# Moving the leftover queries' product into the middle of the two-level stretch, and one late sum behind the last quarter

## The chip, the cores and the metric

The kernel runs on one core of a Trainium2 chip. The metric is the device time of one execution in microseconds (us), the median of several runs. A profiled execution shows when each instruction ran on each engine: PE (matrix products; PEld is its weight loading), DVE (vector sums and products), ACT (copies and functions of one argument), POOL[...] and SP (it issues most transfers, as DMA queue).

## The reference

Two blocks follow each other. The first is a linear attention with a norm over each head's 64 values, the second a multiplicative feed-forward network:

```python
kv  = np.einsum('bhsd,bhse->bhde', k, v)
o   = np.einsum('bhsd,bhde->bhse', q, kv)
rms = np.sqrt(np.mean(o * o, axis=-1, keepdims=True) + 1e-06)
o   = o / rms * g_norm
x   = o.transpose(0, 2, 1, 3).reshape(B * S, H * D)
a, b = x @ w1, x @ w2
out = ((a * b) @ w3) @ w_out
```

B = 8 batches, H = 8 heads, S = 576 tokens, D = 64. So x has 4608 rows of 512 columns; w1 and w2 are 512 x 1024, w3 is 1024 x 1024 and w_out 1024 x 512. Everything is float32.

## The kernel before

**Groups.** The 4608 tokens are worked in nine groups of 512. Groups 0 to 7 take the first 512 tokens of batches 0 to 7. The 64 tokens that each batch has beyond 512 are collected into group 8: the *leftover* queries of two batches at a time make one block of 128 rows, so the leftover product is made at each odd batch (1, 3, 5, 7), for that batch and the one before it. The groups run in the order 0 to 6, 8, 7. w3 and w_out are multiplied into one matrix at the start.

**Stages of a group.** While group T is in the network, the attention of batch T+1 is made for the next group, in small pieces between its products. The network's first product (x with w1 and w2) is cut into four blocks of columns, p0 to p3. The matrix products use Strassen's scheme with Winograd's sums: seven products of quarters instead of eight, with sums of quarters made on DVE before and after. In groups 4, 5, 6, 8 and 7 the blocks p0 and p1 are done together with two levels of the scheme (`gates_of_two`, "the stretch of the two levels"): a first half with w1 and a second half with w2, seven outer products of seven matmuls each. The order there is p2, two-level stretch, p3, then the projection (`project_twice`, the product with the folded matrix, also with two levels). A call `between()` after certain products runs the next piece of attention: pieces 0 and 1 in p2, 2 and 3 after the third and the sixth product of the first half, 4 and 5 likewise in the second half, 6 and 7 in p3.

**Memory of the products.** PE writes into eight banks: five in the pool `ps_mm` ("mm") for the network, three in `ps_at` ("at") for the attention. The two-level stretch holds all five of "mm". An outer product fills two banks; of the seven, several accumulate into banks that ACT has copied out (`keep`, L994 and L995) or DVE has added up (`add`, L999 and L1000) just before; `finish` (L1011 to L1016) makes the sums of a quarter.

**Attention pieces.** `begin_kv` (L340) makes the keys' product, `product` (L430) the main queries' product, followed by `norm`: ACT squares (L390), DVE reduces (L399), ACT takes the root (L403), DVE takes the reciprocal (L405) and multiplies (L408). From batch 5 on (`b > FIRST_OF_TWO`) the buffer of the squares is a single one. `product_left` (L449) is the leftover queries' product; its norm has 256 columns instead of 512. `x_left_by_dma` turns the result: POOL copies (L299), a transposing DMA on SP's queue (L301), POOL copies back (L311). The operand of `product_left`, qT_left, comes the same way, with ACT copies, in the slot after the fourth product of the first half.

**Before the change, for batches 5 and 7**, `product_left` is piece 6, in p3 of groups 4 and 6, with one bank of "at" and one of "mm". Its two squares are issued at once into two halves of one buffer; the reduces and the root run when DVE has finished the quarter c12 of p3, the reciprocal and the multiplies behind the quarter c22. For batches 1 and 3 all of the norm runs at once.

**The sums behind p3's quarters.** The quarters c12, c22, c11 and c21 of p3 come in this order (L860, L861; c21 L857). Behind each of them `following` holds the sums that the projection needs. `sum_ab_two` makes four sums for the blocks p0 and p1: two (L1044, L1045) right behind the two-level stretch, the third (L1046, c12 from c11) and the fourth (L1047, called s4) in `following`. `sum_ab` does the same for p3 (L773, L774), and `sum_inner` (L1141 to L1145) makes the second level's sums for the projection's products in turn.

**What sets the order.** PE, POOL and SP run in the order of the program. In p3 and in the projection DVE does as well (in groups 8 and 7 from the two-level stretch on); elsewhere a scheduler places DVE's and ACT's instructions. Each engine works through its own queue in order.

Of the kernel before, what the change touches and what calls it, by code (L numbers as in the profile page):

```python
# [12 lines left out]
FP32 = mybir.dt.float32  # L13
# [3 lines left out]
AF = mybir.ActivationFunctionType  # L17
ALU = mybir.AluOpType
AX = mybir.AxisListType
# [3 lines left out]
def kernel(  # L23
# [32 lines left out]
    nc = tc.nc  # L56
    PSUM = bass.MemoryType.PSUM
    P = 128

    B, H, S, D = q.shape  # L60
# [4 lines left out]
    FIRST_OF_TWO = 4  # L65
    NH = KF // 2
    J = 4
    G = J * P
# [7 lines left out]
    work = ctx.enter_context(tc.tile_pool(name="work", bufs=2))  # L76
    ps_mm = ctx.enter_context(tc.tile_pool(name="ps_mm", bufs=5, space=PSUM))
# [6 lines left out]
    def bank(pool, tag):  # L84
        return pool.tile([P, 512], FP32, name=tag, tag=tag)
# [169 lines left out]
    def all_of(steps):  # L255
        for _ in steps:
            pass
# [63 lines left out]
    def attention(b):  # L321
# [53 lines left out]
            to = st["qT"].rearrange("p r t -> p (r t)")  # L375
            return turn_by_dma([src], to, src, [to], copy or q_copy)

        def norm(o_ps, dsts, squares_first=False):

            n, w = len(o_ps), o_ps[0].shape[1]  # L380
            inv = work.tile([P, n, w // D], FP32, name="inv")
            sq = []

            def square(i):
                if squares_first and i:
                    sq.append(sq[0][:, w:2 * w])
                else:
                    at = 0 if b > FIRST_OF_TWO else i
                    sq.append(work.tile([P, G], FP32, name=f"sq{at}", bufs=1))
                nc.scalar.activation(sq[i][:, 0:w], o_ps[i], AF.Square)  # L390

            if squares_first:
                for i in range(n):
                    square(i)
                yield
            for i in range(n):
                if not squares_first:
                    square(i)
                nc.vector.tensor_reduce(  # L399
                    out=inv[:, i], in_=sq[i][:, 0:w].rearrange("p (h d) -> p h d", d=D), axis=AX.X, op=ALU.add  # L400
                )
            yield
            nc.scalar.activation(inv, inv, AF.Sqrt, scale=1.0 / D, bias=eps_col)  # L403
            yield
            nc.vector.reciprocal(inv, inv)  # L405
            for i in range(n):
                m, k = dsts[i].shape[1:3]
                nc.vector.tensor_tensor(  # L408
                    out=dsts[i],
                    in0=o_ps[i].rearrange("p (m k d) -> p m k d", k=k, d=D),  # L410
                    in1=inv[:, i].rearrange("p (m k) -> p m k", k=k).unsqueeze(3).to_broadcast(
                        [P, m, k, D]
                    ),
                    op=ALU.mult,
                )
# [24 lines left out]
        def product_left():  # L440

            xn = st["left"] = work.tile([P, NP, 2, D], FP32, name="xn_left", bufs=1)

            o_ps = [bank(ps_at, "at"), bank(ps_mm, "mm")]
            for r in range(NP):
                for l in range(2):
                    for e in range(2):
                        rows = slice(e * D, (e + 1) * D)
                        nc.tensor.matmul(  # L449
                            o_ps[e][l * L:(l + 1) * L, r * D:(r + 1) * D],  # L450
                            lhsT=st["qT"][rows, r, l * L:(l + 1) * L],
                            rhs=kv_sb[(b - 1 + l) % 3][rows, e, r, :],
                            start=True,
                            stop=True,
                        )
            o_ps = [t[:, 0:NP * D] for t in o_ps]
            dsts = [xn[:, :, e:e + 1, :] for e in range(2)]
            if b <= FIRST_OF_TWO:
                all_of(norm(o_ps, dsts))
            else:  # L460
                left_norm.append(norm(o_ps, dsts, True))
                next(left_norm[0])

        def turn(r):

# [62 lines left out]
            q_two_by_dma, q_by_dma, q_left_by_dma, x_by_dma, x_part_by_dma, x_left_by_dma, load_ahead,  # L528
        )})

    batches, left_norm = {}, []

    def batch(b):
        if b not in batches:
# [51 lines left out]
    def steps(b):  # L586

        a = batch(b)
        a.start()
        more = b + 1 < B
        fs, ends = ([[] for _ in range(8)] for _ in range(2))

        def turn(i, f, *args, next_group=False):

            t = []

            def begin():  # L600
                t.append(f(*args))
                next(t[0])
                next(t[0])

            fs[i].append((begin,))
            (to_end if next_group else ends[i + 1]).append((lambda: all_of(t[0]),))

        if to_end:

            ends[0] += [(lambda: nc.gpsimd.tensor_copy(tick, late["p5"][:, 0, 0:1]),), *to_end]  # L610
        to_end.clear()
        odd = b % 2
        by_scalar = b > FIRST_OF_TWO
        if b == 1:
            early.extend(a.q_two_by_dma(r) for r in (0, 1))
            q_first = list(early)
            fs[0].append((a.begin_kv, 0, 1))

            def end_first():
                for t in q_first:  # L620
                    with tc.issue_after(copies["kv"].ins):
                        next(t)
                    all_of(t)

            ends[1].append((end_first,))
        fs[1] += [(a.begin_kv, 2, 3), (a.finish, 0)]
        if b == 1:
            last = {}

            def begin(name, behind, f, *args):  # L630
                last[name] = f(*args)
                with tc.issue_after(copies[behind][-1].ins):
                    next(last[name])
                next(last[name])

            def end(name, behind):
                with tc.issue_after(copies[behind][-1].ins):
                    next(last[name], None)
                all_of(last[name])

            fs[2] += [(begin, f"q{r}", "u2", a.q_two_by_dma, r) for r in (2, 3)]
            fs[3] += [
                (begin, "x", "u3", a.x_by_dma, 0, nc.scalar.copy),
                (begin, "left", "u3", a.q_left_by_dma),
            ]
            ends[4] += [(end, "q2", "p1"), (end, "q3", "p5"), (end, "x", "u2")]
            ends[5].append((end, "left", "u3"))
        elif by_scalar:
            turns_by_scalar(b)
        else:  # L650
            turn(1, a.q_two_by_dma, 2, 3)
            turn(2, a.x_by_dma, 0)
            if odd:
                turn(1, a.q_left_by_dma)
        second = 5 if b == 1 else 4
        if more:
            fs[second].append((batch(b + 1).begin_kv, 0, 1))
        fs[second].append((a.finish, 1))
        if odd:
            fs[6 if by_scalar else second].append((a.product_left,))  # L660
        if b == 1:
            turn(6, a.x_by_dma, 1)
            turn(7, a.x_left_by_dma, next_group=True)
        else:
            if not by_scalar:
                turn(5, a.x_by_dma, 1)
            if odd:
                turn(7 if by_scalar else 5, a.x_left_by_dma, next_group=more or by_scalar)
                if by_scalar and not more:
                    slots["proj", "p5"] = [to_end.pop()]  # L670
        if more and not by_scalar:
            turn(7 if b == 1 else 5, batch(b + 1).q_two_by_dma, 0, 1, next_group=True)
        if more:
            fs[7 if odd else 0].append((load_q_left, b + 1))
        return iter([lambda s=e + f: [f(*args) for f, *args in s] for e, f in zip(ends, fs)])
# [728 lines left out]
    for n, T in enumerate(groups):  # L1404
# [29 lines left out]
        for p in range(NF):  # L1434
# [3 lines left out]
            if T and p + 1 == NF:  # L1438
                sum_1, sum_2, sum_4, sum_3 = sum_ab(p)
                following = {  # L1440
                    "c12": [], "c22": [sum_1],
                    "c11": [
                        lambda: sum_inner(0, lambda: all_of(f() for f in (sum_2, sum_3))),
                        lambda: sum_inner(1),
                    ],
                    "c21": [sum_4],
                }

                if T in IN_TWO:
                    following["c12"] += [lambda: all_of(next(t) for t in left_norm for _ in range(2)), *of_two[:1]]  # L1450
                    following["c22"] += [lambda: all_of(left_norm.pop()) if left_norm else None, *of_two[1:]]
                if T not in TWICE:
                    in_order = tc.manual_schedule(engines={mybir.EngineType.DVE})
                    in_order.__enter__()
                gates(T, p, between, lambda name: all_of(f() for f in following[name]))
                continue
# [82 lines left out]
```

## Time and profile before

| | us |
|---|---|
| median of 3 runs | 755.9 (755.87 to 755.94) |
| the profiled execution | 757.01 |
| its span, first to last instruction | 754.9 |
| PE busy in it | 744.5 (99%) |
| DVE busy | 635.8 (84%) |
| ACT busy | 322.4 (43%) |
| POOL busy | 85.2 (11%) |

The granted clock of PE is 1.0 of full speed throughout. The stages of three groups, from the chain of waits and the windows of the trace:

| | two-level stretch | length | DVE busy | ACT busy | p3 and projection |
|---|---|---|---|---|---|
| group 4 (leftover of batch 5) | 407.09 to 431.57 | 24.48 | 19.84 | 20.33 | to 467.91 |
| group 5 (no leftover) | 482.61 to 507.09 | 24.48 | 19.66 | 18.62 | to 541.07 |
| group 6 (leftover of batch 7) | 555.76 to 578.93 | 23.17 | 19.85 | 19.30 | to 615.34 |

Group 6 has no keys' product in that stretch (batch 8 doesn't exist), which is 1.31 us in groups 4 and 5. A line of the chain or of the timeline begins with its start and its length in us; "x24" is a number of records (a float32 matmul leaves two), and "[0.91 <-DVE ab L861]" means that the engine sat idle for 0.91 us and what ended the idle time. Busy time of PE is no proof of full speed, since the ends of matmuls are modelled.

### The profile page before, as it was taken

How to read it: one execution, taken by the hardware profiler on the slowest of the kernel's cores; microseconds unless marked ns; L12 is line 12 of the kernel's file. 1: busy time of each engine (PE TensorE's matmuls, PEld its weight loads, DVE VectorE, ACT ScalarE, POOL GpSimd, SP SyncE). 2: the span in 40 equal slices, each digit the busy share in tenths (PEclk: the TensorE clock that was granted, in tenths of full speed). 3: DMA queues.
4: the chain of work that ended last, by engine and by line, in shares of the span. 5: the costliest groups of instructions: out<-in, count | busy, mean ns of one | idle time of the engine just before them, and what ended most of it. 6: DMA issues, size and time to landing. Idle time of an engine off the chain costs nothing.

```text
span 754.9 us, 15615 instructions
## 1 busy us (share of the span) xinstructions
PE 744.5 (99%) x6155; PEld 659.2 (87%) x6155; DVE 635.8 (84%) x1301; ACT 322.4 (43%) x558; POOL 85.2 (11%) x83
## 2 busy tenths in 40 slices
PE   7999999999999999999999999999999999999998
PEld 5455788888899889988999989999999899999997
DVE  6977999638888669877798899889979897998897
ACT  6777787312322332223225753565367323222321
POOL 0000000222520442053201000100000100000000
PEclk9999999999999999999999999999999999999999
DMA  8996954349997947697578987798656763365354
GB/s 310 344 334 189 273 154 113 85 94 280 329 298 256 251 121 206 227 247 214 151 232 217 267 211 268 207 265 258 250 136 207 190 209 128 147 212 186 121 204 138
DMA packets 155245, 160.94 MB, mean 213 GB/s; under 512 B 87076, under 2 KB 140068, under 8 KB 155172
## 3 DMA queue, kind: packets, MB, share of 16 engines
q1 hardware_dynamic: 152720, 145.52, 65.6%
q10 hardware_dynamic: 2452, 14.42, 5.7%
q8 instruction: 49, 0.80, 0.4%
q14 instruction: 24, 0.20, 0.1%
HBM read 121.90 MB, written 20.71 MB: 189 GB/s over the span
## 4 chain that ended last, share of the span: by engine, by line
PE 91%; DVE 5%; DMA 2%; ACT 1%; issue 0%; SPq 0%; DVEq 0%; ACTq 0%
PE mm L720 42%; PE mm L1183 21%; PE mm L974 15%; PE mm L699 7%; PE at L340 2%; PE at L430 2%; DMA raw<-in_moe_w_out_dram 1%; DVE c L860 1%; PE at L686 1%; DMA raw<-w3o_l 1%; DVE ab L861 1%; DMA raw<-in_moe_w_dram 1%; PE at L1234 0%; DVE inv L399 0%; DVE raw L896 0%
## 5 line engine op out<-in xcount | busy, mean ns | idle before, releaser
L720 PE MATMUL mm<-xT,w_sb 128*128 128x256 f32 x576 | 132.2, 379 | 0.0
L720 PEld LDWEIGHTS mm<-xT,w_sb 128*128 128x128 f32 x576 | 108.7, 190 | 14.8 <-issue 0.5
L720 PE MATMUL mm<-xc,ws 128*128 128x256 f32 x416 | 94.8, 380 | 0.6 <-ACT p L733 0.6
L720 PEld LDWEIGHTS mm<-xc,ws 128*128 128x128 f32 x416 | 78.8, 190 | 12.4 <-ACT p L733 1.8
L699 PE MATMUL mm<-chunks,ab 128*128 128x512 f32 x128 | 60.1, 602 | 1.2 <-DVE chunks L174 1.2
L733 ACT COPY u<-mm 128x512 f32<-128x512 f32 x46 | 27.0, 587 | 74.3 <-PE mm L720 59.6
L733 ACT COPY p<-mm 128x512 f32<-128x512 f32 x54 | 31.5, 586 | 51.5 <-PE mm L720 45.4
L1183 PE MATMUL mm<-w3o_sb,ab 128*128 128x128 f32 x368 | 49.3, 276 | 2.1 <-DVE ab L861 1.9
L720 PE MATMUL mm<-xc,w_sb 128*128 128x256 f32 x208 | 50.0, 383 | 0.0
L1183 PEld LDWEIGHTS mm<-w3o_sb,ab 128*128 128x128 f32 x368 | 45.5, 192 | 3.3 <-DVE ab L861 2.3
L1194 ACT COPY u<-mm 128x512 f32<-128x512 f32 x23 | 13.5, 586 | 81.4 <-DVE raw L1207 48.0
L1183 PE MATMUL mm<-w3o_sb,raw 128*128 128x128 f32 x372 | 48.1, 275 | 0.0
L720 PE MATMUL mm<-xT,ws 128*128 128x256 f32 x192 | 46.0, 382 | 0.0
L1183 PEld LDWEIGHTS mm<-w3o_sb,raw 128*128 128x128 f32 x372 | 44.8, 192 | 0.0
L399 DVE TENSOR_REDUCE inv<-sq 128x8 f32<-128x512 f32 (+1 forms) x40 | 23.9, 627 | 24.5 <-ACT sq L390 24.5
L720 PEld LDWEIGHTS mm<-xc,w_sb 128*128 128x128 f32 x208 | 38.8, 190 | 5.6
L861 DVE TENSOR_TENSOR ab<-c 128x256 f32<-128x256 f32 x78 | 41.3, 529 | 2.1
L699 PEld LDWEIGHTS mm<-chunks,ab 128*128 128x128 f32 x128 | 21.8, 190 | 23.6 <-issue 15.3
L720 PEld LDWEIGHTS mm<-xT,ws 128*128 128x128 f32 x192 | 36.0, 190 | 5.1
L855 ACT COPY c<-mm 128x256 f32<-128x256 f32 x26 | 9.7, 372 | 68.5 <-PE mm L720 68.5
L974 PE MATMUL mm<-ws,w3o_sb 128*128 128x128 f32 x250 | 38.5, 275 | 0.0
L297 POOL COPY xT<-xn 128x1024 uint16<-128x1024 uint16 x14 | 17.3, 1264 | 152.4 <-DVE xn L408 152.4
(249 smaller groups left out, 1630.5 us busy)
## 6 DMA issues: line engine op xcount, KB each, us to landing
w3o_sb<-w3o_l SPq DMA_DIRECT2D x18, 896.0 KB, 5.7
raw<-in_moe_w_dram SPq DMA_DIRECT2D x31, 512.0 KB, 7.2
raw<-w3o_l SPq DMA_DIRECT2D x15, 896.0 KB, 4.9
w3o_sb<-w_l SPq DMA_DIRECT2D x15, 896.0 KB, 5.0
w3o_sb<-w3o_l ACTq DMA_DIRECT2D x14, 896.0 KB, 4.6
k_sb<-in_k_dram SPq DMA_DIRECT2D x32, 256.0 KB, 4.3
v_sb<-in_v_dram SPq DMA_DIRECT2D x32, 256.0 KB, 4.8
q_sb<-in_q_dram SPq DMA_DIRECT2D x32, 256.0 KB, 3.8
```

The lines of the kernel that those rows point to most:

```text
L297: copy(to, src.rearrange("p a n w -> p w a n"))
L340: nc.tensor.matmul(kv_ps[e * D:(e + 1) * D, r - rs[0], :], lhsT=k_sb[:, e, cols] if j < J else kl[:, 2 * r + e, :], rhs=v_sb[:, e, cols] i ...
L399: nc.vector.tensor_reduce(out=inv[:, i], in_=sq[i][:, 0:w].rearrange("p (h d) -> p h d", d=D), axis=AX.X, op=ALU.add)
L430: nc.tensor.matmul(o_ps[l][tokens, n * D:(n + 1) * D], lhsT=qT[r][rows, e, i, tokens], rhs=kv_b[rows, e, r, :], start=True, stop=True,)
L699: nc.tensor.matmul(sums_ps[half][m], lhsT=w3T[half, c][:, m, :], rhs=chunks[:, c, 1, :], start=(c == 0), stop=(c == KF - 1),)
L720: nc.tensor.matmul(ps[:, u, :], lhsT=lhsT(a_name, u, c), rhs=rhs(b_name, c),  start=(u == 0 and c == 0 and to is None), stop=(c == chunks ...
L733: copies.setdefault(name, []).append(nc.scalar.copy(t, ps))
L855: copied = nc.scalar.copy(c, one[:, 0, :])
L861: nc.vector.tensor_mul(dst, c[:, 0, :], c[:, 1, :])
L974: nc.tensor.matmul(ps[place // 4][:, place % 4, :], lhsT=x, rhs=y, start=new and place // 4 not in seen, stop=True, skip_group_check=True,)
L1183: nc.tensor.matmul(to[:, i, :], lhsT=x[:, c, :], rhs=y[:, c, :], start=new and place // 4 not in seen, stop=(c == 1), skip_group_check=True,)
L1194: nc.scalar.copy(t[:, 0:4], ps[0])
```

## The change

1. For batches 5 and 7 `product_left` becomes piece 3, after the sixth product of the first half of the two-level stretch, instead of piece 6. Both its banks are of "at". Its norm runs at once, as for the other batches, and no longer in parts behind c12 and c22; both squares use the same place, so the second waits for the first reduce.
2. `x_left_by_dma` begins at piece 5 instead of 7. Its end is, for batch 5, piece 0 of the next group as before, and for batch 7 piece 6 of the same group instead of a slot in the projection.
3. In groups 4, 5, 6, 8 and 7 the third sum of `sum_ab_two` (L1046) moves from behind c12 to behind c22, and the fourth (L1047) from behind c22 to behind c21, the last quarter.

```diff
-        def norm(o_ps, dsts, squares_first=False):
+        def norm(o_ps, dsts):
 
             n, w = len(o_ps), o_ps[0].shape[1]
             inv = work.tile([P, n, w // D], FP32, name="inv")
-            sq = []
-
-            def square(i):
-                if squares_first and i:
-                    sq.append(sq[0][:, w:2 * w])
-                else:
-                    at = 0 if b > FIRST_OF_TWO else i
-                    sq.append(work.tile([P, G], FP32, name=f"sq{at}", bufs=1))
-                nc.scalar.activation(sq[i][:, 0:w], o_ps[i], AF.Square)
-
-            if squares_first:
-                for i in range(n):
-                    square(i)
-                yield
             for i in range(n):
-                if not squares_first:
-                    square(i)
+                sq = work.tile([P, G], FP32, name=f"sq{0 if b > FIRST_OF_TWO else i}", bufs=1)[:, 0:w]
+                nc.scalar.activation(sq, o_ps[i], AF.Square)
                 nc.vector.tensor_reduce(
-                    out=inv[:, i], in_=sq[i][:, 0:w].rearrange("p (h d) -> p h d", d=D), axis=AX.X, op=ALU.add
+                    out=inv[:, i], in_=sq.rearrange("p (h d) -> p h d", d=D), axis=AX.X, op=ALU.add
                 )
             yield
...
-            o_ps = [bank(ps_at, "at"), bank(ps_mm, "mm")]
+            o_ps = [bank(ps_at, "at"), bank(*((ps_at, "at") if b > FIRST_OF_TWO else (ps_mm, "mm")))]
...
-            dsts = [xn[:, :, e:e + 1, :] for e in range(2)]
-            if b <= FIRST_OF_TWO:
-                all_of(norm(o_ps, dsts))
-            else:
-                left_norm.append(norm(o_ps, dsts, True))
-                next(left_norm[0])
+            all_of(norm(o_ps, [xn[:, :, e:e + 1, :] for e in range(2)]))
...
-            fs[6 if by_scalar else second].append((a.product_left,))
+            fs[3 if by_scalar else second].append((a.product_left,))
...
-                turn(7 if by_scalar else 5, a.x_left_by_dma, next_group=more or by_scalar)
-                if by_scalar and not more:
-                    slots["proj", "p5"] = [to_end.pop()]
+                turn(5, a.x_left_by_dma, next_group=more)
...
                 if T in IN_TWO:
-                    following["c12"] += [lambda: all_of(next(t) for t in left_norm for _ in range(2)), *of_two[:1]]
-                    following["c22"] += [lambda: all_of(left_norm.pop()) if left_norm else None, *of_two[1:]]
+                    following["c22"].append(of_two[0])
+                    following["c21"].append(of_two[1])
```

More of the change, by code (lines that the diff above doesn't have):

```diff
@@ L529, in attention @@
         )})
-    batches, left_norm = {}, []
+    batches = {}
     def batch(b):
```

## The prediction

> **What bounds the kernel now.** I read the page's busy row first: PE is busy 744.5 of 754.9 us, DVE 635.8, ACT 322.4. So only a place where PE waits can give time back. Then the chain of waits, in order of time: in the late groups it is PE without a break, except in two places, 439 to 448 us (group 4) and 587 to 596 us (group 6). These are the two groups that carry the leftover product of an odd batch (5 and 7). Here the chain around the first, and, below the second break, group 5, which carries none (columns: start us, us, what):
>
> ```profile
> 431.57 5.18 PE mm L720 x24
> ...
> 437.38 1.94 PE mm L720 x8
> ...
> 443.47 0.76 DVE xn_left L408 x2
> 444.23 0.60 DVE raw L1047
> ...
> 448.44 19.47 PE mm L1183 x172
> ```
> ```profile
> 507.09 12.09 PE mm L720 x56
> 519.18 21.88 PE mm L1183 x196
> 541.07 4.10 PE mm L720 x19
> ```
>
> The reader should not take the nine microseconds of DVE for a loss: PE works under most of them. Group 5 is the yardstick. From the start of the last block (p3) to the next group it takes 541.07 - 507.09 = 33.98; group 4 takes 467.91 - 431.57 = 36.34, group 6 615.34 - 578.93 = 36.41. The excess is 2.36 + 2.43 = 4.79 us. PE's timeline splits it, group 4 first, then group 5:
>
> ```profile
> 442.59 1.89 PE L720 MATMUL mm<-xc,w_sb 128*128 128x256 f32 x8
> 444.32 0.83 PE L1183 MATMUL mm<-w3o_sb,ab 128*128 128x128 f32 x6
> 446.06 0.94 PE L1183 MATMUL mm<-w3o_sb,ab 128*128 128x128 f32 x6 [0.91 <-DVE ab L861]
> ...
> 448.99 1.28 PE L1183 MATMUL mm<-raw 128*128 128x128 f32 x10
> ```
> ```profile
> 517.29 1.89 PE L720 MATMUL mm<-xc,w_sb 128*128 128x256 f32 x8
> 519.02 1.50 PE L1183 MATMUL mm<-w3o_sb,ab 128*128 128x128 f32 x12
> ...
> 522.14 1.06 PE L1183 MATMUL mm<-raw 128*128 128x128 f32 x8
> ```
>
> The last block's last product starts 442.59 - 431.41 = 11.18 after the block's first matmul in group 4, 517.29 - 506.93 = 10.36 in group 5: the leftover product costs PE 0.82. The projection's first product takes 448.99 - 444.32 = 4.67 against 522.14 - 519.02 = 3.12: a wait of 1.55. It waits for L861 and then for sums that DVE reaches late, since the leftover norm (two reduces, reciprocal, two multiplies) stands before them.
>
> **What the Trainium skill says.** "PSUM — Partial Sum Buffer", section Engine vs sequencer instructions: ScalarE's and VectorE's queues are strict FIFO, and matmuls start and complete in program order. The trace agrees: the leftover squares of group 4 start at 439.21, only when two queue copies (437.32 to 439.31) end. The same page, section PSUM bank collisions, asks that engines be kept apart bank by bank; so a product may enter a bank only when the copy that empties it is done, which decides the second half below. "ScalarE: Activation LUTs", section What ACT_TABLE_LOAD costs, puts a switch of table sets at about 2.66 us; the trace shows none here: Sqrt at 408.35 is followed by a copy at 408.56. "SBUF — State Buffer", section Who interferes with whom: a VectorE operation with two SBUF inputs contends with GpSimd's reads. The trace agrees: L1145 takes 0.88 instead of 0.42 beside the x_left copies at 596.29.
>
> **The change part by part.** The built order shows that, line numbers apart, only the following moves.
>
> *The product.* Its 16 matmuls leave p3 (-0.82 in each of groups 4 and 6) and come between the sixth and seventh product of the first half. There they cost 0.82 again if I take p3's price. The lower bound is the main product's rate, 64 records in 1.09, so 32 in 0.55; nothing below it, since the work stays on the binding engine. I take 0.8. Its operand is ready: the ACT copy of qT_left ends at 414.91, the sixth product at 416.19. So are two banks of the attention pool: the first norm read them until 410.27.
>
> *The norm on ACT.* This is the tight place. ACT between, before the change (group 4):
>
> ```profile
> 414.81 1.99 ACT L297 COPY xT<-xn 128x1024 uint16<-128x1024 uint16 x2
> 417.39 0.59 ACT L994 COPY p<-mm 128x512 f32<-128x512 f32 x1 [0.59 <-PE mm L974]
> 418.06 0.48 ACT L995 COPY p<-mm 128x384 f32<-128x384 f32 x1
> 418.44 1.17 ACT L311 COPY qT<-q_sb 128x1024 uint16<-128x1024 uint16 x1
> 419.50 0.59 ACT L994 COPY u<-mm 128x512 f32<-128x512 f32 x1
> ```
>
> Now both squares stand before the first L994 and Sqrt behind its L995. Both squares share one buffer, so the second waits for the first reduce. First square: PE ends the product near 416.95, square until 417.35. Reduce: DVE has its earlier sums until 417.98, so 417.98 to 418.39. Second square 418.48 (0.09 is the hand-over seen at 406.65). L994 from 418.77, L995 from 419.25, Sqrt 419.62, L311 419.83, and the L994 of the second half's first product 420.89 to 421.48: 1.4 later than before. Behind it waits the second half's third product, which accumulates in that bank. It began at 420.88; pushed by 0.8 it comes at 421.7. Slack 0.2, so I book 0.1 in all; bounds 0 and, if ACT loses another copy's time (0.59), 0.4 in each group. Before that nothing binds: bank 0 is free at 419.4 and needed at about 421.
>
> *The norm on DVE.* Two reduces, reciprocal and two multiplies are 0.33 + 0.33 + 0.2 + 0.34 + 0.34 = 1.5 at their spacing, and some waiting for Sqrt; the second half's first L999 goes from 420.64 to about 422.2. Its bank is next needed at 425.1 + 0.8, by the fourth product. The lag dies at the next norm: DVE idles 1.68 before 425.81 and 0.92 before 427.41. The banks that the next main product needs are free at about 421.2; it comes at 424.5 in group 4, 423.2 in group 6.
>
> *What disappears.* p3 and the projection of groups 4 and 6 get group 5's queues: -0.82 and -1.55 (1.61 in group 6). What is late next there is what binds in group 5: L1145 ends at 521.42 and PE needs it at 521.70, 0.28 of cover. Those are the sums behind c11, and they don't move.
>
> *The late sum, in groups 4 to 8.* L1046 goes from behind c12 to behind c22, L1047 from there to behind c21. c22's L860 waits for PE's fifth product in any case (515.76), so DVE idles 0.6 between and what stands behind c21 comes 0.6 later. Cover: the first of these sums ends at 524.13 and is used at 526.61; the later ones have 1.9 or more. At the end of the kernel DVE's last but one sum starts at 750.27, the last at 751.60 when PE is done: 0.92 idle takes the 0.6. Cost 0; without this cover 0.3 at the end. It can also gain: if a group comes to p3 late on DVE, the 0.6 hole takes the lag up.
>
> *POOL and SP.* POOL's turn copy of xn_left (1.28) starts near 421 instead of 444.44, its DMA transpose stands on SP ahead of the three loads of projection weights, which wait for PE until 428.25; by then POOL is done. So SP isn't held, and the later load of the fourth weights, at 447.76 behind the transpose now, comes earlier. In group 6 POOL's x_left copies (1.65) fall into the second half and slow two or three DVE sums by some 0.4 each; DVE idles 0.92 near there. Cost 0, without cover 0.3.
>
> **Sum.** -4.79 + 1.6 + 0.1 = -3.1. The profiled execution took 757.01, so 753.9; the median lies 1.1 below it: 755.9 - 3.1 = 752.8.
>
> **Rivals.**
> A, the forecast: 752.8; own range 752.2 (product at 0.55 twice: -3.7) to 753.6. For it: group 5 shows the same queues without a wait. 0.72.
> B: ACT's queue slips further and the second half's third product waits 0.5 to 1.2 in each group: 753.8 to 755.2, say 754.3. For it: slack of 0.2 after a chain of seven steps. Against: every step has a duration from a row. 0.13.
> C: DVE doesn't get rid of its lag, and the projection's first product waits as before: 755.9 + 0.1, 756.0. For it: DVE is busy 19.84 of the 24.48 us of the stretch, and 1.5 is added. Against: the idle 2.6 above. 0.09.
> D, slower: the second square waits for the reduce, and behind it on ACT stand the copies that empty the banks. Each microsecond that DVE reaches the first reduce later then moves the third product of the second half, beyond its slack of 0.2. It decides from 1.75 us per group on (the slack and half of 3.1): a second square after 420.2. At 2.6 us, 755.9 - 3.1 + 2 x (2.6 - 0.2) = 757.6. Against: the sums ahead of the reduce are those that end at 417.98 now, and nothing that they wait for moves. 0.06.
>
> **How the numbers follow.** About 0.2% (1.5 us) is what a measurement of this kernel can tell from no change, so faster means below 754.4: A and 0.08 of B, 0.80. Within: the rest of B and C, 0.14. Slower: D, 0.06. The range 752.0 to 754.4 leaves out 0.20.
>
> **What would show it.** Right: in groups 4 and 6 p3 12.09 and the projection 21.88, as in group 5; no wait at L861; the stretch of the two levels 24.48 + 0.8 and 23.17 + 0.8. Wrong: a wait of PE before the second half's third product (B), the wait at the projection's first product still there (C), squares or L994 after 421 (D), or a product whose matmuls cost more than 0.82 in the middle.

## The result and the profile after

| | before | after |
|---|---|---|
| median | 755.92 us (755.70 to 758.03, 6 runs) | 753.10 us (752.18 to 753.69, 6 runs) |
| profiled execution | 757.01 | 753.10 |
| its span | 754.9 | 751.3 |
| group 4, start of p2 to the next group's | 75.52 | 74.05 |
| group 5 | 73.16 | 73.15 |
| group 6 | 74.27 | 72.66 |
| groups 8 and 7, to the start of the last projection | 114.01 | 114.01 |

The ratio of the times is 0.9958, 95% interval 0.9945 to 0.9971: the changed kernel is faster. The groups' lengths are read from the chain of waits as in the prediction. Groups 4 and 6 became 3.08 us shorter together; the span fell by 3.6. Another 0.54 lies ahead of group 4, where the change moves nothing: group 4 starts at 391.85 instead of 392.39, and over all the kernels below, which share their instructions up to there, it starts anywhere between 390.85 and 392.94. So the group lengths, not the spans, are compared from here on. Each is read from one profiled execution. How closely they can be compared is shown by group 5: it takes 73.15 or 73.16 in every kernel below except e6 with two sums. Behind group 6 the kernels differ only in e2 and in e6 with two sums.

The chain of waits after, in groups 4 and 6 (start us, us, what); most lines moved up by some twenty, L720 is L699, L1183 is L1162, L974 is L953 and L449 is L435:

```profile
406.54 9.38 PE mm L953 x84
415.92 0.62 PE at L435 x32
416.54 6.53 PE mm L953 x56
...
431.92 12.09 PE mm L699 x56
444.01 21.88 PE mm L1162 x196
...
563.12 0.62 PE at L435 x32
563.75 6.45 PE mm L953 x56
...
577.73 12.09 PE mm L699 x56
589.82 21.88 PE mm L1162 x196
```

PE's chain has no break. p3 takes 12.09 and the projection 21.88 in both groups, group 5's lengths; the wait for L861 (now L840) in the projection's first product and the wait behind it are gone. In their place the stretch of the two levels has the leftover product in it: 431.92 - 406.54 = 25.38 in group 4 (24.48 + 0.90), 577.73 - 553.74 = 23.99 in group 6 (23.17 + 0.82).

The tight place, ACT's timeline of group 4 between the product and the second half (L384 square, L973 a copy that empties a bank, L389 root):

```profile
416.59 0.39 ACT L384 ACTIVATE sq<-at 128x256 f32<-128x256 f32 x1 [0.34 <-PE at L435]
418.22 0.39 ACT L384 ACTIVATE sq<-at 128x256 f32<-128x256 f32 x1 [1.24 <-DVE p L990]
418.50 0.58 ACT L973 COPY p<-mm 128x512 f32<-128x512 f32 x1
...
419.33 0.32 ACT L389 ACTIVATE inv<-inv,eps_col 128x8 f32<-128x8 f32 x1
...
420.59 0.60 ACT L973 COPY u<-mm 128x512 f32<-128x512 f32 x1
```

ACT sits idle for 1.24 us before the second square, which can't overwrite the buffer until DVE has reduced the first one (417.43 to 417.84); the trace puts the end of the wait down to L990, the instruction behind that reduce, and in group 6 to the reduce itself. The last copy ends at 421.19, and the third product of the second half starts at 421.26: 6.53 for the stage instead of 6.45 is a wait of 0.08.

And DVE in p3 of group 4 (L839 is the sum for a quarter):

```profile
438.93 0.69 DVE L839 TENSOR_TENSOR c<-mm,u 128x512 f32<-128x512 f32 x1 [0.18 <-PE mm L699]
439.65 0.42 DVE L840 TENSOR_TENSOR ab<-c 128x256 f32<-128x256 f32 x1
440.60 0.69 DVE L839 TENSOR_TENSOR c<-p,mm 128x512 f32<-128x512 f32 x1 [0.52 <-PE mm L699]
```

This is the hole that the moved sum leaves: DVE comes in time and waits 0.52 us for c22's product. In group 6 it comes late, c12's L839 starts with no idle time, and c22's follows without that wait: the hole has taken up the lag. The same two in group 6:

```profile
585.12 0.69 DVE L839 TENSOR_TENSOR c<-mm,u 128x512 f32<-128x512 f32 x1
...
586.41 0.69 DVE L839 TENSOR_TENSOR c<-p,mm 128x512 f32<-128x512 f32 x1
```

### The profile page after: what moved, and what is told of

Its sections match the earlier page's. It is cut to its first block, busy times and chain, and to the rows that moved or that the text cites. A ratio compares the mean times of both kernels' runs of the same rounds, so it can differ in the third digit from the quotient of the medians.

```text
span 751.3 us, 15612 instructions
## 1 busy us (share of the span) xinstructions
PE 743.1 (99%) x6155; PEld 659.0 (88%) x6155; DVE 636.4 (85%) x1301; ACT 322.2 (43%) x558; POOL 84.6 (11%) x83
## 4 chain that ended last, share of the span: by engine, by line
PE 96%; DMA 2%; DVE 2%; ACT 1%; issue 0%; SPq 0%; ACTq 0%
PE mm L699 45%; PE mm L1162 23%; PE mm L953 15%; PE mm L678 7%; PE at L340 3%; PE at L416 2%; DMA raw<-in_moe_w_out_dram 1%; PE at L665 1%; DMA raw<-in_moe_w_dram 0%; PE at L1213 0%; PE at L435 0%; PE at L359 0%; DVE c L839 0%; DVE chunks L174 0%; DVE inv L385 0%; DVE raw L875 0%
## 5 line engine op out<-in xcount | busy, mean ns | idle before, releaser
L699 PE MATMUL mm<-xT,w_sb 128*128 128x256 f32 x576 | 132.2, 379 | 0.0
L699 PEld LDWEIGHTS mm<-xT,w_sb 128*128 128x128 f32 x576 | 108.7, 190 | 14.8 <-issue 0.5
L699 PE MATMUL mm<-xc,ws 128*128 128x256 f32 x416 | 94.8, 380 | 0.4 <-ACT p L712 0.4
L699 PEld LDWEIGHTS mm<-xc,ws 128*128 128x128 f32 x416 | 78.8, 190 | 12.1 <-ACT p L712 1.5
L699 PE MATMUL mm<-xc,w_sb 128*128 128x256 f32 x208 | 50.0, 383 | 0.0
L1162 PE MATMUL mm<-w3o_sb,ab 128*128 128x128 f32 x368 | 48.6, 275 | 0.0
L1162 PE MATMUL mm<-w3o_sb,raw 128*128 128x128 f32 x372 | 48.1, 275 | 0.0
L699 PE MATMUL mm<-xT,ws 128*128 128x256 f32 x192 | 45.8, 381 | 0.0
L1162 PEld LDWEIGHTS mm<-w3o_sb,ab 128*128 128x128 f32 x368 | 45.4, 192 | 0.4
L1162 PEld LDWEIGHTS mm<-w3o_sb,raw 128*128 128x128 f32 x372 | 44.8, 192 | 0.0
L699 PEld LDWEIGHTS mm<-xc,w_sb 128*128 128x128 f32 x208 | 38.9, 190 | 5.5
L840 DVE TENSOR_TENSOR ab<-c 128x256 f32<-128x256 f32 x78 | 40.7, 522 | 2.1
L699 PEld LDWEIGHTS mm<-xT,ws 128*128 128x128 f32 x192 | 36.1, 190 | 5.0
L953 PE MATMUL mm<-ws,w3o_sb 128*128 128x128 f32 x250 | 38.5, 275 | 0.0
```

The source lines that it names most:

```text
L699: nc.tensor.matmul(ps[:, u, :], lhsT=lhsT(a_name, u, c), rhs=rhs(b_name, c),  start=(u == 0 and c == 0 and to is None), stop=(c == chunks ...
L840: nc.vector.tensor_mul(dst, c[:, 0, :], c[:, 1, :])
L953: nc.tensor.matmul(ps[place // 4][:, place % 4, :], lhsT=x, rhs=y, start=new and place // 4 not in seen, stop=True, skip_group_check=True,)
L1162: nc.tensor.matmul(to[:, i, :], lhsT=x[:, c, :], rhs=y[:, c, :], start=new and place // 4 not in seen, stop=(c == 1), skip_group_check=True,)
```

## The experiments

All lengths from the chain of waits, in us; "ratio" is to the kernel before, run beside it on the same chip, with its 95% interval. Medians of different rows can come from different chips, so the ratios are what compares them.

| kernel | group 4 | group 6 | median | ratio |
|---|---|---|---|---|
| the changed kernel | 74.05 | 72.66 | 753.10 | 0.9958 (0.9945 to 0.9971) |
| e1, change without the late sums | 74.06 | 72.90 | 753.33 | 0.9964 (0.9952 to 0.9977) |
| e2, late sums alone | 74.92 | 73.80 | 755.57 | 0.9993 (0.9985 to 1.0001) |
| e4, product in the second half | 74.96 | 74.02 | 755.51 | 0.9991 (0.9985 to 0.9998) |
| e3, two buffers' halves for the squares | 73.97 | 73.17 | 753.10 | 0.9958 (0.9945 to 0.9972) |
| e5, 3 more ACT copies | 74.32 | 72.66 | 753.32 | 0.9956 (0.9941 to 0.9971) |
| e5, 9 more ACT copies | 74.87 | 73.20 | 755.01 | 0.9982 (0.9974 to 0.9990) |
| e5, 20 more ACT copies | 75.90 | 74.23 | 756.46 | 1.0001 (0.9993 to 1.0010) |
| e6, 1 more DVE sum | 74.05 | 72.89 | 753.22 | 0.9955 (0.9940 to 0.9970) |
| e6, 2 more DVE sums | 74.64 | 73.60 | 756.36 | 1.0001 (0.9992 to 1.0010) |
| e7, e3 with ACT's copies of x_left | 73.97 | 73.61 | 754.57 | 0.9974 (0.9964 to 0.9985) |
| e8, e3 with x_left late | 73.97 | 73.46 | 753.63 | 0.9964 (0.9950 to 0.9978) |
| e9, changed kernel with x_left late | 74.05 | 73.21 | 753.82 | 0.9961 (0.9948 to 0.9973) |

### Which part brings the gain: e1 and e2

e1 is the changed kernel with the sums left where they were:

```diff
-                    following["c22"].append(of_two[0])
-                    following["c21"].append(of_two[1])
+                    following["c12"].append(of_two[0])
+                    following["c22"].append(of_two[1])
```

> The leftover product moves as in the change; L1046 and L1047 stay behind c12 and c22. Theory (the move alone brings the gain, the late sum is neutral where the product is gone from p3): 753.0 us, within 0.5 of the changed kernel; groups 4 and 6 show p3 12.09 and projection 21.88. Rival (the hole behind c12 is needed to take up the lag that the norm leaves on DVE): a wait of PE at the projection's first product of groups 4 and 6, 0.3 us or more each, so 753.6 or more.

e2 is the kernel before with the sums moved, and the product and its norm where they were:

```diff
-                    following["c12"] += [lambda: all_of(next(t) for t in left_norm for _ in range(2)), *of_two[:1]]
-                    following["c22"] += [lambda: all_of(left_norm.pop()) if left_norm else None, *of_two[1:]]
+                    following["c12"] += [lambda: all_of(next(t) for t in left_norm for _ in range(2))]
+                    following["c22"] += [lambda: all_of(left_norm.pop()) if left_norm else None, of_two[0]]
+                    following["c21"].append(of_two[1])
```

> The leftover product stays in p3; only L1046 and L1047 move to c22 and c21. Theory (DVE's queue ahead of the projection's first product is what makes PE wait, so each 0.6 us sum taken out of it shortens the wait by 0.6): the wait of 1.55 falls to 0.95 in groups 4 and 6, 754.7 us. Rival (the late sum is neutral everywhere, as the prediction booked it): 755.9.

e1 has the whole gain in group 4 and lacks 0.24 us in group 6. There the sum L1025 is back behind c12, where DVE is late already. DVE's timeline of e1 in group 6, and PE's:

```profile
585.95 0.68 DVE L1025 TENSOR_TENSOR ab<-ab 128x512 f32<-128x512 f32 x1
...
591.78 0.42 DVE L1124 TENSOR_TENSOR ab<-ab 128x256 f32<-128x256 f32 x1
```
```profile
592.25 0.71 PE L1162 MATMUL mm<-w3o_sb,ab 128*128 128x128 f32 x4
```

The sum at L1124 ends at 592.20 and the projection's next product starts at 592.25. So the product's move, with the earlier x_left that e1 keeps, makes the change; e9 below takes the two apart. The late sum adds 0.24 in one group, which the timer can't tell. Alone on the kernel before, the late sum shortens groups 4 and 6 by 0.60 and 0.47, since the projection's first product waits less. But group 8 loses 0.23 of it again in its first block p2, which takes 12.32 instead of 12.09, so 0.84 is left in the trace; the timer's interval for e2 reaches to no change.

### The same move to another place: e4

```diff
-            fs[3 if by_scalar else second].append((a.product_left,))
+            fs[5 if by_scalar else second].append((a.product_left,))
...
-                turn(5, a.x_left_by_dma, next_group=more)
+                turn(7 if by_scalar else 5, a.x_left_by_dma, next_group=more or by_scalar)
+                if by_scalar and not more:
+                    slots["proj", "p5"] = [to_end.pop()]
```

> The leftover product comes after the sixth product of the second half instead of the first half. Theory (the place must have two free banks and a DVE that idles before p3): PE waits about 0.9 us for the bank that the main norm still reads, and the norm's 1.5 us of DVE fall into p3, whose cover is about 1.0; about 1.4 in each of groups 4 and 6, so 755.7. Rival (any place before c12 will do): 753.0.

Most of the gain is gone: groups 4 and 6 are 0.91 and 1.36 us longer than in the changed kernel. The chain of e4 in group 4:

```profile
428.84 0.16 DVE inv L391
...
429.78 0.70 DVE xn L394
...
430.61 0.69 PE at L435 x30
```

The product waits for the banks of "at", which the main norm (L391, L394) still reads: 1.3 us of PE in the two groups by the list of waits. The loss lies mostly in the two-level stretch: all of it in group 4 (26.29 instead of 25.38), and 0.99 in group 6. The 0.36 that group 6 loses behind the stretch can't be told apart from x_left, which e4 must also start late and which alone costs 0.55 there (e9 below). After the first half's sixth product those banks are free (its first norm, in the working above, read them until 410.27). The place, not only the leaving of p3, makes the gain.

### The second square: e3

Both squares go into the two halves of one buffer, ahead of the reduces:

```diff
-                sq = work.tile([P, G], FP32, name=f"sq{0 if b > FIRST_OF_TWO else i}", bufs=1)[:, 0:w]
-                nc.scalar.activation(sq, o_ps[i], AF.Square)
+                if b > FIRST_OF_TWO and w < G:
+                    if i == 0:
+                        both = work.tile([P, G], FP32, name="sq0", bufs=1)
+                        for j in range(n):
+                            nc.scalar.activation(both[:, j * w:(j + 1) * w], o_ps[j], AF.Square)
+                    sq = both[:, i * w:(i + 1) * w]
...
```

> The changed kernel with both squares written into two halves of one buffer, so that the second doesn't wait for the first reduce. Theory (ACT's queue is tight but costs at most 0.1 us in group 4): the copy that empties the first product's bank of the second half ends about 1 us earlier, the 0.08 us goes, 753.0, no difference that can be measured. Rival (waits on ACT cost more than the chain shows): 752.4 or less.

In group 4 the wait of 0.08 goes, 6.45 for 6.53: this is the price at which my slower rival's wait exists. Group 6 became 0.51 longer, which I had not expected. DVE's timeline of e3 there, then that of the changed kernel, then POOL's of the changed kernel:

```profile
572.18 1.18 DVE L1002 TENSOR_TENSOR ab<-ab,c 128x512 f32<-128x512 f32 x1
573.29 0.67 DVE L392 TENSOR_REDUCE inv<-sq 128x8 f32<-128x512 f32 x1
```
```profile
572.25 0.69 DVE L995 TENSOR_TENSOR ab<-ab,c 128x512 f32<-128x512 f32 x1
572.86 0.68 DVE L385 TENSOR_REDUCE inv<-sq 128x8 f32<-128x512 f32 x1
```
```profile
572.84 1.28 POOL L311 COPY x_left<-xn_left 128x512 uint16<-128x512 uint16 x2 [3.88 <-DMA xn_left<-qT_left]
```

In e3 POOL's copies of x_left come at 572.15 and fall on a sum with two inputs in SBUF, which takes 1.18 instead of 0.69; in the changed kernel they come at 572.84 and fall on a reduce, which isn't slowed. "SBUF — State Buffer", section Who interferes with whom, in the Trainium skill says the same: two SBUF inputs contend with POOL's reads, a reduce never does. The trace agrees, 1.18 against 0.68. e7 and e8 test whether that is the half microsecond.

### Taking POOL's copies away: e7, e8, e9

e7 is e3 with ACT instead of POOL for the two copies that bring x_left back from its transpose in the last batch (`nc.scalar.copy` at L311; the copy into the transpose stays on POOL). e8 is e3, and e9 the changed kernel, with x_left begun at piece 7 and ended in the projection for the last batch, as before the change (the second part of e4's diff). In e9 POOL's copy into the transpose runs at 568.01, about as in the changed kernel (567.92); it is the two copies back that move, from 572.84 to 589.22.

> The kernel of e3 (both squares ahead of the sums of squares) with the two copies of the leftover queries at the end of the last batch's group made by ScalarE instead of GpSimd. Theory (the half microsecond that e3 lost in group 6 came from GpSimd's copies that fell on a VectorE sum with two SBUF inputs and held it up by 0.5 us): group 6 comes back to 6.45 us for its second half with no wait, 72.6 us for the group, 753.0 in all or 0.1 less than the changed kernel. Rival (ScalarE's new order is what delays the second square): group 6 stays 0.5 longer, 753.5.

> The kernel of e3 with x_left_by_dma begun at piece 7 and, for the last batch, ended in the projection, as before the change; GpSimd's two copies so leave the second half of group 6. Theory (these copies, where they fall on a VectorE sum with two SBUF inputs, cost e3 its half microsecond in group 6; e7 could not tell, since ScalarE paid for the copies): group 6 comes to 72.7 us or less instead of 73.17, the sum at L1002's place takes 0.69 instead of 1.18, group 4 stays at 73.97; 753.0 to 753.1 in all, 0.1 below the changed kernel's trace. Rival (the delay comes from ScalarE's order with both squares first): group 6 stays at 73.1 to 73.2.

> The changed kernel with the same step alone: x_left_by_dma begun at piece 7 and ended in the projection for the last batch. Theory (in the changed kernel GpSimd's copies fall on a reduce, which they don't slow, so moving them brings nothing; its earlier start is worth nothing either): group 4 at 74.05 and group 6 at 72.66 as in the changed kernel, 753.1. Rival (the earlier start of x_left_by_dma is part of the gain, for the SP queue or VectorE): group 4 or 6 longer by 0.2 or more.

The times missed, and the traces say why. In e7 the sum at L1002's place takes 0.69 again, but ACT waits 1.47 us for the transfer at the head of its queue and then copies for 1.25, with the square for the main norm behind. So e7 told nothing of the half microsecond. In e8 the sum takes 0.69 and the second half of group 6 runs without loss. From the main queries' product to p3 it takes 7.45 us, as in the changed kernel, and 7.73 in e3. DVE's sum in e8, then PE's two starts in the changed kernel, in e3 and in e8:

```profile
571.95 0.69 DVE L1004 TENSOR_TENSOR ab<-ab,c 128x512 f32<-128x512 f32 x1
```
```profile
570.12 1.16 PE L416 MATMUL at<-kv_sb,qT 64*64 64x64 f32 x64
...
577.57 1.89 PE L699 MATMUL mm<-xT,w_sb 128*128 128x256 f32 x8
```
```profile
569.89 1.16 PE L423 MATMUL at<-kv_sb,qT 64*64 64x64 f32 x64
...
577.62 1.89 PE L706 MATMUL mm<-xT,w_sb 128*128 128x256 f32 x8
```
```profile
569.65 1.16 PE L423 MATMUL at<-kv_sb,qT 64*64 64x64 f32 x64
...
577.10 1.89 PE L708 MATMUL mm<-xT,w_sb 128*128 128x256 f32 x8
```

That settles it: POOL's copies, not ACT's order, held e3's second half up. The rest of e3's half microsecond lies behind it, in p3 (12.23 instead of 12.09) and in the projection (21.96 instead of 21.88). But the copies now come in the projection, where they fall on sums that are late in any case. DVE's and PE's timelines of e9, where nothing else differs from the changed kernel:

```profile
589.41 0.75 DVE L842 TENSOR_TENSOR ab<-c 128x256 f32<-128x256 f32 x1
590.20 0.77 DVE L1122 TENSOR_TENSOR raw<-ab 128x256 f32<-128x256 f32 x1
```
```profile
592.95 0.71 PE L1164 MATMUL mm<-w3o_sb,ab 128*128 128x128 f32 x4 [0.29 <-DVE ab L1126]
```

Each of the two sums takes 0.42 in the changed kernel, and group 6 of e9 is 0.55 longer. The changed kernel's two:

```profile
589.25 0.42 DVE L840 TENSOR_TENSOR ab<-c 128x256 f32<-128x256 f32 x1
589.71 0.42 DVE L1120 TENSOR_TENSOR raw<-ab 128x256 f32<-128x256 f32 x1
```

So the earlier place of x_left, which I had booked at nothing, is worth 0.55 us of group 6's gain.

### How much slack ACT has: e5

Small ACT copies, whose result isn't used, behind the root and ahead of the second half's copies:

```diff
+        if b % 2:
+            for i in range(3):
+                at((0, 6), nc.scalar.copy, extra[:, i:i + 1], eps_col)
```

> The changed kernel with three small ScalarE copies added in every group of a two-level tile, between the square root behind the second square and the second half's first copy of xT; their results are not used. Theory (my prediction's term: after the move ScalarE's queue in the second half has no slack, 0.08 us of wait in group 4 and next to none in group 6): at about 0.2 us each (the spacing of the square root's neighbours) 0.6 us are put ahead of the copies that the second half's third product waits for; the wait of that product grows from 0.08 to about 0.6 in group 4 and from nothing to about 0.5 in group 6, and the time from 753.1 to about 754.2. Rival (the queue still hides a microsecond or more, since the leftover queries' product is long enough): no new wait, 753.1.

> The same with nine such copies, 1.8 us in each group. Theory: the wait grows by the full 1.8 less a slack of at most 0.2, in both groups, and nothing takes it up behind: about 756.5, which is slower than the kernel before the change. Rival (slack of a microsecond or more): at most 0.8 a group, 754.7 or less. A second reading is the slope between three and nine copies: 2.3 us for six copies in two groups if the slack is used up by three, less if it is not.

> Twenty of the small ScalarE copies. Three and nine of them put 0.25 and 0.82 us ahead of the copies that the third product waits for (0.09 each); twenty put 1.84. Theory (no slack in group 4, 0.28 in group 6, the rest arrives at the end undiminished): group 4 74.05 + 1.84 = 75.9, group 6 72.66 + 1.56 = 74.2, so 3.4 more than the changed kernel, 756.5, about the time of the kernel before: my slower rival's point of decision of 1.75 us a group. Rival (something behind takes a part of it up): 755.5 or less.

The first two expectations had the wrong price: such a copy is 0.20 us long, but the next starts 0.09 after it. ACT's timeline with nine, and the list of PE's weight loads that waited (total, times, longest) with twenty:

```profile
420.42 0.32 ACT L389 ACTIVATE inv<-inv,eps_col 128x8 f32<-128x8 f32 x1
420.62 0.93 ACT L524 COPY extra<-eps_col 128x1 f32<-128x1 f32 x9
421.45 1.17 ACT L311 COPY qT<-q_sb 128x1024 uint16<-128x1024 uint16 x1
```
```profile
PEld mm L957 <- ACT u L977: 3.3, 2, 1.8
```

From root to L311 it is 1.03 instead of 0.21, so nine copies add 0.82, three 0.25 and twenty 1.85. Group 4 grew by 0.82, 0.27 and 1.85: no slack at all. Group 6 grew by 0.54, 0 and 1.57: a slack of 0.28 by both larger ones. Nothing behind takes a part of it up, and at twenty copies the time is the kernel's before.

### How much slack DVE has in p3: e6

e6 adds one or two sums of 512 columns behind c12, in the groups with the two-level stretch. The edit for two:

```diff
+                    spare, c12, c22 = ab_sums[2][:, 0:2], ab[0][:, 0:2, 1, :], ab[1][:, 0:2, 1, :]
+                    following["c12"] += [lambda: nc.vector.tensor_add(spare, c12, c22)] * 2
```

> The changed kernel with one more sum of VectorE behind the p3 piece c12 in every two-level and one-level group, 0.6 us long, into columns that are written again later. Theory (behind c12 VectorE has a hole of 0.5 us in a group that comes in time, and the last sum of the projection has a cover of about 0.28): the sum fills the hole; nothing in groups 4, 5, 8 and 7, about 0.25 us in group 6, where the hole already takes up VectorE's lag: 753.3. Rival (VectorE is on no path in p3, any sum there is free): 753.1 without a change in group 6.

> The same with two such sums. Theory: 1.2 us are 0.7 more than the hole and 0.4 more than hole and cover together, so about 0.4 us in each of four groups and 0.85 in group 6, where there is no hole: together about 2.4, 755.5, with the projection's first products waiting for VectorE's late sum. Rival (free): 753.1.

One more sum costs nothing in groups 4 and 5, and 0.23 in group 6. Two cost 0.59 in group 4, 0.60 in group 5, 0.94 in group 6 and 1.2 in groups 8 and 7 together: 3.3 where I expected 2.4. The chain of the kernel with two, in group 4:

```profile
439.31 0.61 DVE raw L1432
...
439.94 0.69 DVE raw L1432
440.63 0.61 DVE c L839
...
446.25 19.47 PE mm L1162 x172
```

The two take 440.63 - 439.31 = 1.32, not 1.2. Less the hole of 0.52 and the 0.59 that arrive at the end, 0.21 is left as the cover of the projection's first sums, where I had read 0.28. In group 4 of the changed kernel DVE is busy for 32.01 of the 33.98 us of p3 and projection. So 1.97 are idle, and yet only one more sum of 0.6 fits in at this place: the hole and the cover decide, not the busy share.

## Why the prediction was right

**The excess of p3 and projection, -4.79.** After the change these stages take 33.98 us in groups 4 and 6, so 2.36 and 2.43 went: the term as it stood. Group 5 was the right yardstick. In group 6 this took the earlier x_left as well (see POOL below).

**The product again, +1.6.** It cost 0.82 in each group, 1.64. Its own line shows 0.62. The other 0.20 appears in the products behind it: six products take 9.38 ahead of it, 1.563 each, and four take 6.45 behind it instead of 6.25. The lower bound of 0.55, taken from the main product's line alone, was not met. What makes the 0.20 was not tested.

**ACT, +0.1.** 0.08 in group 4, nothing in group 6. Step by step the working was late by up to 0.3: with the 0.54 of the start taken off, the second square was due at 417.94 and came at 418.22, behind L990 instead of behind the reduce (why one instruction later is not settled); the last copy, due to end at 420.94, ended at 421.19. The slack of 0.2 was right as a size, but it lies in group 6 (0.28 by e5), where no keys' product follows; group 4 has none. -4.79 + 1.64 + 0.08 = -3.07, and the groups show -3.08.

**DVE's lag.** The second half's first L978 was due at 421.7 and came at 422.52. I had POOL's copies in mind for group 6 only; in group 4 its turn copy falls on a sum too, which takes 1.14 instead of 0.42. It bound nothing, because DVE's idle time before the next norm's reduces (0.25 and 0.86 left of 1.68 and 0.92) took it up. That is why rival C (the wait stays) did not come.

**The late sum, 0.** Right for the cost: group 5, groups 8 and 7 and the last product are as long as before; the idle time before DVE's last sum fell from 0.92 to 0.52. The gain that I had named as possible and not counted is 0.24, in group 6 (e1).

**POOL and SP, 0.** This was the step with the least ground. The copies of x_left do fall into the second half, but on a reduce, which costs nothing; at their old place they would now cost 0.55 (e9), and 0.45 earlier in the group, in e3, the group is 0.51 longer. The copy into the transpose, L299, fell on a sum in both groups, which the idle time above took up. The zero was right as a sum, in part by luck, and hid a step whose value depends on where in DVE's queue 1.3 us of POOL happen to fall.

**Rival B (ACT slips) and D (slower).** The mechanism of D is there, at 0.08 us. Its point of decision, 1.75 us a group, came out: with 1.85 more on ACT in each group the ratio is 1.0001.

**From the sum to the time.** 753.9 was forecast for the profiled execution, and it took 753.1; 752.8 for the median, which is 753.1. I took the 1.1 us by which the profiled execution lay above the median as a property of the kernel. It isn't one: after the change the two are equal. Half of it, 0.54, is the later start of group 4, ahead of everything that the change moves. For the change itself the trace agrees with the sum (-3.08 for -3.1), and the median moved by 2.82.

No version here beats the changed kernel: the two ratios that are lower (e5 with three copies, e6 with one sum) lie well within its interval and are longer in the trace, as is e3 with the same ratio.

## What to carry to other kernels

When one group of a loop carries an extra piece of work, a group without it tells what the piece costs where it stands, and the stage lengths tell what it would cost elsewhere; look for a place where its banks are free and where the engines behind it have idle time before anything next depends on them. Count slack on each in-order queue separately, down to tenths of a microsecond: here ACT had none in group 4 and 0.28 in group 6, and DVE had room for one sum in a group that comes in time, and for a part of one in group 6. A helper engine's copies belong in such a count, by what they fall upon and not by their own length.

## What the runs showed of the hardware

- POOL copies beside DVE sums with two SBUF inputs made the sums 0.12 to 0.87 us longer (from 0.42 to between 0.54 and 1.17, from 0.69 to 1.18, from 0.28 to 1.15), and left a reduce of 512 columns at 0.68.
- Which of the two began first mattered in the two cases seen. In e3 POOL began at 572.15 and the sum at 572.18, and the sum took 1.18. In e5 with twenty copies the sum began at 575.27 and POOL at 575.40: the sum took 0.69, and POOL's two copies 1.69 instead of 1.28.
- ACT copies of one column are 0.20 us long but 0.09 apart, so a queue of them adds less than half of their length.
- The leftover product's 32 records of 64x64 tiles cost PE 0.82 both in p3 and in the two-level stretch: 0.62 on its own line and the rest around it. On its own line the main product takes 1.09 for 64 of them.
